# V loaded in place, scalings on ACT, f16 halves for the last keys, logits in two parts, fewer routing steps, and a new order of all queues

## The chip, the cores and the metric

The kernel runs on one core of a Trainium2 chip. The metric is the device time of one execution in microseconds. The engines are PE (matmuls; PEld is its loading of weights), DVE (vector), ACT (scalar, activations), POOL (GpSimd) and SP (which issues most DMAs). Each runs its own instructions in order and waits on semaphores for the others.

## The reference

```python
scores = scale * np.matmul(q, k.transpose(0, 1, 3, 2))     # 8 batches, 8 heads, 576 tokens, 64 wide
kth = np.partition(scores, -top_k, axis=-1)[..., -top_k:-top_k + 1]      # top_k = 32
scores = np.where(scores >= kth, scores, -1000000000.0)
attn = np.exp(scores - np.max(scores, axis=-1, keepdims=True))
attn = attn / (np.sum(attn, axis=-1, keepdims=True) + 1e-09)
x = np.matmul(attn, v)                                     # then (8*576, 512)
logits = x @ w_gate                                        # 8 experts
order = np.argsort(-logits.flatten())
for idx in order:                                          # cap = 4608 / 8 = 576
    tok, e = (int(idx) // E, int(idx) % E)
    if assigned[tok] >= 0 or counts[e] >= cap:
        continue
    assigned[tok] = e
    counts[e] += 1
...
out[mask] = np.maximum(x[mask] @ w1[e], 0.0) @ w2[e]       # mask: the tokens of expert e
```

## The kernel before

**Attention.** The work is 32 pairs: a batch and two neighbouring heads. A pair has 2 x 576 queries in nine tiles of 128: tiles 0 to 3 are the first head's first 512 queries, 5 to 8 the second head's, and tile 4 the last 64 queries of both. q and k are scaled and split into an f16 high and low part, so that two f16 matmuls give scores near f32. `prep` does this for a pair ahead: loads (SP), scaling (`scaled`), high and low parts (POOL), transposes by DMA (`turn`, four a pair: K2, K3, Q2, Q1), and for V a load, `scaledv`, `highv` (ACT) and `lowerv` (POOL).

`tile_ops` finds each query's 32nd largest score: PE writes the scores into one of three PSUM buffers `s`; DVE takes the eight largest of each of six pieces of 96 (L221) and from those, in five steps, the first 24 (L224 to L228); `sign` on ACT marks the scores above the 24th and sums the marks into `acc`; PE adds a large number there (`move(off)`); DVE fills eight more columns (`fill`, L238) and takes the next eight (`next8`, L239); PE moves the scores back (`move(back)`); `relu` on ACT leaves a mask that frees the buffer.

`soft` makes the weights for one tile, keys on the partitions: mask and scores again on PE, `expo` on ACT, f16 high and low parts on POOL (L293, L296). These cover the first 512 keys. `tail` does the last 64 keys for eight tiles at once (`E4`) and the corner of the last queries and last keys (`E4r`). `values` multiplies with V, whose column 65 of constants gives the sum; one group of tiles at a time, of tile 4 with f32 weights. A division on DVE and a scaling on ACT write x. After the four pairs of a batch, `logits` transposes x and multiplies with the gate, and x goes to DRAM.

The order of each engine's queue is set by `Plan`, a list scheduler: every operation has a due time (`O`, with a distance `PER` a tile), an assumed duration `d`, and a window for each engine (`WIN`). What it chooses becomes the program's order; on the chip each engine keeps it. `verdict` then sums checks of `acc`, `cuts` and the logits into `flags`; a branch skips the repair `redo`.

**Experts.** `moe()` uses a second plan. Expert by expert, a search finds the threshold above which the chosen expert has 576 tokens: six steps of comparing on DVE (`g`, L671), counting on PE (L674), adding up (L677, L680, L684), comparing with 576 (`okb`, L687) and taking the best expert (L688, L689). Then the tokens are listed (`enlist`), gathered from DRAM (`bring`: POOL gathers, ACT and DVE split into f16 parts, SP transposes by DMA into `xT`), and two layers of matmuls follow (L856, L880), while the next experts are routed and their weights `wr` loaded by SP and split by ACT and DVE. The first search is `p==0`.

Of the kernel before, what the change touches and what calls it, by code (L numbers as in the profile page):

```python
# [99 lines left out]
def attention(tc, q,k,v,w_gate,x_out,L,flags, pairs):  # L100
# [3 lines left out]
    with ExitStack() as ctx:  # L104
# [37 lines left out]
        O=dict(ld=-16.716, hk=-154.219, hq=68.962, gk=-25.585, gk2=47.53, gq=-130.711, gq2=-89.008, tk=27.44, tk3=-68.629, tq=-75.928, lv=6.408, hv=31.03, gv=101.34, gv2=-15.258, S=-52.406, c0=108.15, c1=-33.761, c2=85.771, c3=-0.645, c4=16.105, c5=34.028, nt=11.747, wb=-7.377, k0=-35.533, k1=-46.672, k2=-51.349, k3=-28.446, k4=23.429, nb=22.884, sg=24.883, wm=-11.243, y8=-71.884, j8=28.216, rl=-16.239, m1=-12.137, m2=-85.93, q2=64.018, t0=37.709, t1=91.29, t2=-2.439, td=-2.756, ex=108.922, eh=53.858, el=35.874, u0=34.296, ud=-71.623, ue=-103.988, uh=-45.573, ul=-62.63, x0=29.098, xe=-69.485, xh=-60.222, xl=9.443, v0=45.124, v1=49.568, v2=49.224, vd=-1.065, vn=-40.84, vs=19.481, lg=53.386, lgd=6.924, l1=-50.298, l2=2.231, l3=-3.333, hg=96.246)  # L142
# [4 lines left out]
        def prep(n):  # L147
# [53 lines left out]
            P["lds"]=at(t0+O["lv"],loadv,[l],e="D",d=2.2,late=2.0)  # L201
            P["vs"]=s3=at(t0+O["gv"],scaledv,[P["lds"],q2]+p3,e="G",d=.95)
            a=at(t0+O["hv"],lambda: highv(0),[s3],e="A",d=.3); a=at(t0+O["hv"]+O["hg"],lambda: highv(1),[a],e="A",d=.3)
            P["vready"]=at(t0+O["gv2"],lowerv,[a],e="G",d=1.13)
        def tile_ops(P,i):
# [32 lines left out]
            def fill(): V.tensor_scalar(D["s"][:,576:584],tab,acc[:,col],P["st"][:,i,23:24],op0=ALU.is_lt,op1=ALU.mult)  # L238
# [21 lines left out]
            if i%3==2:  # L260
                i0=i-2
                def most():
                    t=wk.tile([128,3],F32,tag="m3",name="m3",bufs=2)
                    G.tensor_scalar(t,P["st"][:,i0:i0+3,0],1.0/QS,0.0,op0=ALU.mult,op1=ALU.add)
                    G.tensor_scalar(P["nq"][:,1,i0:i0+3,64],t,1.0,0.0,op0=ALU.mult,op1=ALU.add)
                    G.tensor_tensor(P["nq"][:,1,i0:i0+3,65],t,P["nq"][:,1,i0:i0+3,64],op=ALU.subtract)
                def q2(): nc.sync.dma_start_transpose(P["Q2t"][:,i0:i0+3,:],P["nq"][:,1,i0:i0+3,:].rearrange("p a b -> p (a b)"))
                a=at(t0+O["m1"],most,[P["mx"][j] for j in range(i0,i+1)],e="G",d=.6); P["q2"][i0//3]=at(t0+O["q2"],q2,[a],e="D",d=.65,late=2.0)
        def soft(P,i):
# [27 lines left out]
            p=tp=at(t0,masks,[P["rel"][i],P["q2"][i//3]],take="pt",e="P",d=.225)  # L297
# [12 lines left out]
        def tail(P):  # L310
# [36 lines left out]
        def values(P):  # L347

            n=P["n"]; hp=P["hp"]; last=[]
            for g in (0,1,2):  # L350
# [4 lines left out]
                def dot(j,part,D=D,g=g,begin=begin):  # L355
                    if j==0 and part==0: begin()
                    av=D["av"]; vt,vh,vl=P["vt"],P["vh"],P["vl"]
                    h=0 if g==0 else 1
                    if g!=1: e_=P["e"][j if h==0 else 5+j]; out=av[:,j,:]; cs=lambda c: slice(c*128,c*128+128); last=P["e4"][:,j*128:j*128+128]
                    else: h=j; e_=P["e"][4]; out=av[h*64:h*64+64,0,:]; cs=lambda c: slice(c*128+h*64,c*128+h*64+64); last=P["e4r"]  # L360
                    if type(e_) is tuple: seq=[(e_[x][:,cs(c)],v_[:,h,c,:]) for c in range(4) for (x,v_) in ((0,vh),(0,vl),(1,vh))]
                    else: seq=[(e_[:,cs(c)],vt[:,h*5+c,:]) for c in range(4)]
                    seq.append((last,vt[:,h*5+4,:])); N=len(seq)
                    for m_ in (range(N-1) if part==0 else (N-1,)): T.matmul(out,seq[m_][0],seq[m_][1],start=(m_==0),stop=(m_==N-1))  # L364
# [23 lines left out]
        def logits(P):  # L388
            b=P["b"]; n=P["n"]; t0=(n*9+8)*PER+O["lg"]
            fin=[]  # L390
            for c in range(5):
                p=P["done"]
                D={}; w=512 if c<4 else 256
                def turn(c=c,D=D):
                    D["pt"]=ps_t.tile([128,512],F32,tag="pt",name="ptl")
                    for f in range(4 if c<4 else 2): T.transpose(D["pt"][:,f*128:(f+1)*128],P["x"][0][:,c,f*128:(f+1)*128] if c<4 else P["x"][1][:,2*f:2*f+2,:].rearrange("p a d -> p (a d)"),identf)
                def copy(D=D,w=w):
                    D["xT"]=wk.tile([128,512],F32,tag="xT",name="xT",bufs=2); A.activation(D["xT"][:,:w],D["pt"][:,:w],AF.Copy)
                def dot(c=c,D=D):
                    lg=D["lg"]=ps_t.tile([128,512],F32,tag="pt",name="lg"); xT=D["xT"]; o=(b%2)*64  # L400
                    if c<4:
                        for f in range(4): T.matmul(lg[:,:8],xT[:,f*128:(f+1)*128],wg[:,f,:],start=(f==0),stop=(f==3))
                    else:
                        for i_,(g,a) in enumerate(((0,0),(0,1),(1,0),(1,1))): T.matmul(lg[o:o+64,:8],xT[:,g*128+a*64:g*128+a*64+64],wgr[:,g,a,:],start=(i_==0),stop=(i_==3))
                def put(c=c,D=D):
                    o=(b%2)*64
                    if c<4: A.activation(L[:,b*4+c,:],D["lg"][:,:8],AF.Copy)
                    else: A.activation(L[o:o+64,32+b//2,:],D["lg"][o:o+64,:8],AF.Copy)
                t=t0+O["lgd"]*c
                p=at(t,turn,[p],take="pt",e="P",d=.436); tp=p  # L410
                p=at(t+O["l1"],copy,[p],free=[tp],take="xT",e="A",d=.48); tx=p
                p=at(t+O["l2"],dot,[p],take="pt",free=[tx],e="P",d=.9); tp=p
                p=at(t+O["l3"],put,[p],free=[tp],e="A",d=.07); fin.append(p)
            P["fin"]=at(t0,lambda: None,fin)
            P["done"]=p
        def verdict():

# [531 lines left out]
```

## Time and profile before

| | |
|---|---|
| median of 3 runs | 1474.12 us (1472.0 to 1474.5) |
| the profiled execution | 1470.44 us, its span 1468.4 us |
| granted TensorE clock, mean | 0.958 |
| PE busy | 1295.9 us (88%) |
| DVE busy | 1220.3 us (83%) |
| ACT busy | 864.6 us (59%) |
| POOL busy | 877.2 us (60%) |

Busy times are sums over three stages with different limits: attention up to about 955 us, routing up to 1028 us, and experts behind it. The rows below are from stretches of one stage.

### The profile page before, as it was taken

The page shows a single profiled execution, that of the slowest core. Times are in us where ns is not written, and L with a number is a line of the kernel's source. Part 1 is how long each engine was busy: PE and PEld are TensorE (multiplying, and loading weights), DVE is VectorE, ACT ScalarE, POOL GpSimd, SP SyncE. Part 2 cuts the span into 40 slices and gives each one's busy share as a digit, 9 for nine tenths or more (in the row PEclk, how much of TensorE's full clock was granted, in tenths as well). Part 3 has the DMA queues.
Part 4 walks back from the last instruction along what each step waited for, and adds up shares of the span by engine and source line. Part 5 has one row for each costly group of instructions (what it writes and reads, how often), then busy time and mean ns, then how long its engine had stood idle before and what let it go on. Part 6 is the DMA issues. An engine that isn't in the chain of part 4 may idle for free. (4 is left out here: it accounts for less than half of the span.)

```text
span 1468.4 us, 41338 instructions
## 1 busy us (share of the span) xinstructions
PE 1295.9 (88%) x14885; PEld 913.2 (62%) x14886; DVE 1220.3 (83%) x5951; ACT 864.6 (59%) x1922; POOL 877.2 (60%) x1285
## 2 busy tenths in 40 slices
PE   2888998999999999999999899832999999998997
PEld 1666776776776776677677677621655655664663
DVE  4899999999999999999999999658889878887610
ACT  2677777777777777777777787612334424324421
POOL 5688789788788788789879878502043123122211
PEclk9899999999999999999999999955999999999899
DMA  6343363354455445443543452016346346348500
GB/s 130 74 88 78 80 127 84 75 120 91 82 110 97 89 108 84 94 109 77 97 110 83 92 107 46 10 35 170 122 99 198 137 91 198 140 96 271 112 33 33
DMA packets 298149, 149.62 MB, mean 102 GB/s; under 512 B 255440, under 2 KB 280016, under 8 KB 296912
## 3 DMA queue, kind: packets, MB, share of 16 engines
q1 hardware_dynamic: 292048, 128.02, 38.5%
q0 software_dynamic: 5888, 18.88, 4.5%
q8 instruction: 119, 1.95, 0.6%
q14 instruction: 94, 0.77, 0.2%
HBM read 71.34 MB, written 18.87 MB: 61 GB/s over the span
## 5 line engine op out<-in xcount | busy, mean ns | idle before, releaser
L221 DVE MAX8 cd<-s 128x8 f32<-128x96 f32 x1728 | 383.2, 251 | 35.4 <-PE s L218 28.6
L296 POOL TENSOR_TENSOR elm<-F,ehm 128x512 f16<-128x512 f32 x256 | 294.3, 1156 | 6.3
L242 ACT ACTIVATE r<-s,st 128x576 bf16<-128x576 f32 x288 | 213.0, 740 | 98.8 <-PE s L236 93.8
L233 ACT ACTIVATE w<-s,st 128x576 uint16<-128x576 f32 x288 | 213.1, 740 | 95.0 <-DVE st L229 92.9
L895 POOL DMA_INDIRECT out_dram<-ob,idx x40 | 59.0, 1476 | 326.1 <-ACT ob L890 268.2
L239 DVE MAX8 st<-s 128x8 f32<-128x584 f32 x288 | 220.5, 766 | 10.4 <-PE s L236 6.7
L218 PE MATMUL s<-K,Q 128*128 128x512 f16 (+3 forms) x1280 | 195.3, 293 | 28.6 <-DMA Q<-nq 22.3
L856 PE MATMUL ph<-xT,w1h 128*128 128x288 f16 x1024 | 195.8, 289 | 2.0 <-DMA xT<-xs 2.0
L293 POOL TENSOR_SCALAR ehm<-F 128x512 f16<-128x512 f32 x256 | 156.0, 617 | 52.7 <-ACT F L290 52.3
L286 PE MATMUL pt<-Q,K 66*128 66x128 f16 (+1 forms) x1280 | 182.6, 217 | 0.2 <-DMA Q<-nq 0.2
L285 PE MATMUL pt<-Q,K 128*128 128x128 f16 (+1 forms) x1280 | 181.6, 216 | 0.0
L218 PEld LDWEIGHTS <-Q 128*128 128x128 f16 (+1 forms) x1280 | 105.9, 103 | 111.9 <-DMA Q<-nq 22.0
L236 PE MATMUL s<-w,off 128*128 128x512 f16 x576 | 134.1, 290 | 46.8 <-DVE s L238 26.9
L290 ACT ACTIVATE F<-pt 128x512 f32<-128x512 f32 x256 | 150.4, 596 | 20.8 <-PE pt L286 18.5
L856 PE MATMUL ph<-xT,w1l 128*128 128x288 f16 x512 | 147.6, 288 | 0.0
L364 PE MATMUL pv<-vt,E 128*64 128x65 f32 (+1 forms) x1024 | 146.4, 257 | 0.0
L236 PE MATMUL s<-w,back 128*128 128x512 f16 x576 | 120.9, 292 | 23.5 <-DVE st L239 21.7
L865 ACT ACTIVATE hh<-ph 128x288 f16<-128x288 f32 x128 | 52.4, 410 | 146.3 <-PE ph L856 145.4
L285 PEld LDWEIGHTS <-K 128*128 128x128 f16 x1280 | 118.3, 99 | 22.5 <-issue 8.7
L364 PEld LDWEIGHTS <-ehm 128*128 128x128 f16 x2048 | 116.2, 102 | 10.0 <-issue 0.5
L364 PEld LDWEIGHTS pv<-vt,E 128*64 128x64 f32 (+1 forms) x1024 | 113.0, 164 | 14.5 <-issue 3.5
L364 PE MATMUL pv<-vh,ehm 128*128 128x65 f16 x1024 | 120.8, 195 | 0.6 <-ACT F L290 0.6
(252 smaller groups left out, 3271.0 us busy)
## 6 DMA issues: line engine op xcount, KB each, us to landing
wr<-in_moe_w_dram SPq DMA_DIRECT2D x32, 1024.0 KB, 8.2
kn<-in_k_dram SPq DMA_DIRECT2D x64, 128.0 KB, 2.6
qn<-in_q_dram SPq DMA_DIRECT2D x64, 128.0 KB, 2.3
vn<-in_v_dram SPq DMA_DIRECT2D x64, 128.0 KB, 2.3
x<-xb SPq DMA_DIRECT2D x8, 1024.0 KB, 4.8
Q<-nq SPq DMA_TRANSPOSE x160, 3.3
kn<-in_k_dram SPq DMA_DIRECT2D x64, 16.0 KB, 2.3
qn<-in_q_dram SPq DMA_DIRECT2D x64, 16.0 KB, 2.2
```

The lines of the kernel that those rows point to most:

```text
L218: T.matmul(s_ps[rows,a:b_],P[Q][:,qc],P[K][:,h*576+a:h*576+b_],start=(Q=="Q1"),stop=(Q=="Q2"))
L221: V.max(D["cd"][:,c*8:c*8+8],D["s"][:,576*c//NCH:576*(c+1)//NCH])
L233: A.activation(D["w"],D["s"][:,:576],AF.Sign,bias=P["st"][:,i,32:33],scale=(1+2.0**-21),accum_out=acc[:,col])
L236: T.matmul(D["s"][:,a:b_],by,w[:,a:b_],start=False,stop=True,skip_group_check=True)
L239: def next8(): V.max(P["st"][:,i,24:32],D["s"][:,:584])
L242: A.activation(r,D["s"][:,:576],AF.Relu,bias=P["st"][:,i,31:32],scale=-1.0)
L285: T.matmul(o,K2[:,kb:kb+128],Q1[:,qc],start=False,stop=False,skip_group_check=True)
L286: T.matmul(o,K3[0:66,kb:kb+128],Q2[0:66,qc],start=False,stop=(c==3 and h==sub[-1][0]),skip_group_check=True)
L293: G.tensor_scalar(D["eh"],D["E"],1.0,0.0,op0=ALU.mult,op1=ALU.add)
L296: G.tensor_tensor(el,D["E"],D["eh"],op=ALU.subtract); P["e"][i]=(D["eh"],el)
L364: for m_ in (range(N-1) if part==0 else (N-1,)): T.matmul(out,seq[m_][0],seq[m_][1],start=(m_==0),stop=(m_==N-1))
L856: P.matmul(B["ph"][:,:288],a[:,c,fs],xT[:,b+c,cs],start=(i==0),stop=(i==11))
```

## The change

- V is loaded straight into `vt`, whose rows hold 65 floats, without a buffer of its own; its scaling, in place, and those of q and k go from POOL to ACT. `vh` and `vl` now hold all ten blocks.
- The weights of the last 64 keys are split into f16 high and low parts on POOL and multiplied by three f16 matmuls; before, one f32 matmul did it. The f32 weights share the ring `F`. In tile 4 the two heads' f32 matmuls alternate.
- `fill` multiplies by a constant instead of a column.
- `logits` is split: three of four column blocks after a batch's third pair, the rest after the fourth; the results are put, and added, by DVE. `verdict` looks at the logits in four pieces.
- In the first search the counts of all thresholds come from PE directly, without L677, L680 and L684. In all searches a constant row in `okb` takes the place of the matmul with `mone` (L685).
- For the first expert, `bring` transposes on PE and writes `xT` from PSUM by ACT and DVE, instead of by DMA.
- `PER`, `SP`, `WIN` and `O` have new values in both plans, so that the order of all queues is another.

```diff
-        PER=4.6166; SP=1.3822; VP=3; WPB=14; EHB=14
-        WIN={'V': 0.027, 'A': 0.079, 'G': 0.008, 'P': 0.138, 'D': 1.472}
+        PER=3.6791; SP=5.5328; MG=3; WPB=14; EHB=14
+        WIN={'V': 0.009, 'A': 0.159, 'G': 0.0, 'P': 0.097, 'D': 2.593}
...
             def loadv():
-                t=nat["v"]=io.tile([128,9,64],F32,tag="vn",name="vn")
                 for h in range(2):
-                    nc.sync.dma_start(out=t[:,h*4:h*4+4,:],in_=v[b,2*hp+h,0:512,:].rearrange("(p c) d -> p c d",c=4))
-                    nc.sync.dma_start(out=t[64*h:64*h+64,8,:],in_=v[b,2*hp+h,512:576,:])
...
+                    nc.sync.dma_start(out=vt[:,h*5:h*5+4,0:64],in_=v[b,2*hp+h,0:512,:].rearrange("(p c) d -> p c d",c=4))
+                    nc.sync.dma_start(out=vt[64*h:64*h+64,h*5+4,0:64],in_=v[b,2*hp+h,512:576,:])
+            def scaledv(): A.activation(vt[:,:,0:64],vt[:,:,0:64],AF.Copy,scale=VS)
+            def highv(h): A.activation(vh[:,h*5:h*5+5,0:64],vt[:,h*5:h*5+5,0:64],AF.Copy)
+            def lowerv(): G.tensor_tensor(vl[:,:,0:64],vt[:,:,0:64],vh[:,:,0:64],op=ALU.subtract)
...
-                G.tensor_scalar(s,nat[nm],QS,0.0,op0=ALU.mult,op1=ALU.add)
+                A.activation(s,nat[nm],AF.Copy,scale=QS)
...
-            P["lds"]=at(t0+O["lv"],loadv,[l],e="D",d=2.2,late=2.0)
-            P["vs"]=s3=at(t0+O["gv"],scaledv,[P["lds"],q2]+p3,e="G",d=.95)
...
+            P["lds"]=lv=at(t0+O["lv"],loadv,[l]+p3,e="D",d=2.2,late=2.0)
+            P["vs"]=s3=at(t0+O["gv"],scaledv,[lv],e="A",d=.66)
...
-            def fill(): V.tensor_scalar(D["s"][:,576:584],tab,acc[:,col],P["st"][:,i,23:24],op0=ALU.is_lt,op1=ALU.mult)
+
+            def fill(): V.tensor_scalar(D["s"][:,576:584],tab,acc[:,col],2.0**40,op0=ALU.is_lt,op1=ALU.mult)
...
+            p=te=at(t0+O["u0"]+O["ue"],expo4,[p],free=[tp],take="F",e="A",d=.48)
+            p=P["te4"]=at(t0+O["u0"]+O["uh"],hi4,[p],take="E4",e="G",d=.59)
+            P["e4op"]=at(t0+O["u0"]+O["ul"],lo4,[p],free=[te],e="G",d=1.115)
...
-                    seq.append((last,vt[:,h*5+4,:])); N=len(seq)
...
+                        else: seq=[(P["e4"][x][:,js],v_[:,h*5+4,:]) for (x,v_) in ((0,vh),(0,vl),(1,vh))]
+                        for m_,(a,b_) in enumerate(seq): T.matmul(out,a,b_,start=(part==0 and m_==0),stop=(part==1 and m_==2))
+                    else:
+
+                        e_=P["e"][4]
+                        for c in range(5):
+                            for h in range(2):
+                                a=e_[:,c*128+h*64:c*128+h*64+64] if c<4 else P["e4r"]
+                                T.matmul(av[h*64:h*64+64,0,:],a,vt[:,h*5+c,:],start=(c==0),stop=(c==4))
...
+            if P["hp"]==2: logits(P,0)
+            if P["hp"]==3:
+                P["done"]=at(P["done"]["t"]+.001,lambda: None,[P["done"],Ps[n-1]["fin"]])
...
+                            if p==0:
+                                for j in range(q*n,q*n+n): P.matmul(D_["pn"][:T,:E],D_["g"][:,j,:],D_["ohb"][:,j,:],start=(j==0),stop=(j==NT-1))
...
-                        P.matmul(D_["pn"][:,16:16+E],onesb[:1,:],mone,start=True,stop=False,skip_group_check=True)
...
+                if p==0:
+                    B={}
+                    def turn(j=j,n=n,B=B):
+                        if j==0: e["xT"]=new(sm,[128,8,CAP],F16,"xT")
+                        B["pt"]=new(ps,[128,512],F32,"ph",4).rearrange("p (f n) -> p f n",f=4)
+                        for f in range(4): P.transpose(B["pt"][:,f,:n],xgs[j][:n,f*128:f*128+128],ident[:n,:n])
+                    def hi(j=j,n=n,B=B): A.activation(e["xT"][:,0:4,j*128:j*128+n],B["pt"][:,:,:n],AF.Copy,scale=SX)
+                    def lo(j=j,n=n,B=B): V.scalar_tensor_tensor(e["xT"][:,4:8,j*128:j*128+n],B["pt"][:,:,:n],SX,e["xT"][:,0:4,j*128:j*128+n],op0=ALU.mult,op1=ALU.subtract)
```

Three places of the new order follow. On PE, in `values` of one pair in the middle of the attention stage (`E` are tile 4's f32 weights, `E4` and `E4r` those of the last keys, `s` a tile's scores), there stood:

```order
L236 MATMUL s_18398<-w_18526,off_144 128x512
L364 MATMUL pv_18479<-vt2_185,E4_18323 128x65
L364 MATMUL pv_18576<-vt2_185,E_18217 64x65 x4
L236 LDWEIGHTS off_144
L236 MATMUL s_18398<-w_18526,off_144 128x64
L364 MATMUL pv_18576<-vt2_185,E4r_18354 64x65
L364 MATMUL pv_18576<-vt2_185,E_18217 64x65 x4
L236 LDWEIGHTS back_146
L236 MATMUL s_18398<-w_18526,back_146 128x512
```

The same work in a pair of the change:

```order
L370 LDWEIGHTS eh4_11893
L370 MATMUL pv_12081<-vh1_183,eh4_11893 128x65
L370 LDWEIGHTS eh4_11893
L370 MATMUL pv_12081<-vl1_187,eh4_11893 128x65
L370 LDWEIGHTS el4_11900
L370 MATMUL pv_12081<-vh1_183,el4_11900 128x65
L377 MATMUL pv_12182<-vt1_179,E_11743 64x65 x8
L377 MATMUL pv_12182<-vt1_179,E4r_11971 64x65 x2
L231 LDWEIGHTS off_144
L231 MATMUL s_12002<-w_12194,off_144 128x512
```

The f32 matmul with `E4` has become three f16 ones with their weight loads, and tile 4's ten f32 calls stand in one piece; before, moves of a tile stood between them.

On DVE, at the end of the attention stage (`vc` to `good` are the check of `acc`, `fin` that of the logits `L`), the order before was:

```order
L424 SCALAR_TENSOR_TENSOR vok<-vc,vok 128x288
L425 SCALAR_TENSOR_TENSOR vok<-vc,vok 128x288
L426 SCALAR_TENSOR_TENSOR vok<-cuts,vok 128x288
L428 TENSOR_REDUCE good<-vok 128x32
L430 TENSOR_TENSOR fin<-L 128x288
```

And in the change:

```order
L428 COPY L<-lg 64x8
L432 TENSOR_TENSOR L<-lg,L 128x32
L433 TENSOR_TENSOR L<-lg,L 64x8
L439 TENSOR_SCALAR vc<-acc 128x288
L440 TENSOR_SCALAR vr<-vc 128x288
L441 TENSOR_SCALAR vr<-vr 128x288
L442 TENSOR_TENSOR vok<-vr,vc 128x288
L443 SCALAR_TENSOR_TENSOR vok<-vc,vok 128x288
```

The logits' puts are now on DVE, and they stand ahead of the eight instructions that check `acc`.

On SP, at the last experts (`wr` are weights, `xT<-xs` the transposes of expert 6's input), the order before was:

```order
L787 DMA wr<-in_moe_w_dram 128x2x1024
L840 DMA_TRANSPOSE xT<-xs 128x8x128
L787 ISA
L787 DMA wr<-in_moe_w_dram 128x4x512
L840 DMA_TRANSPOSE xT<-xs 128x8x128 x3
L840 DMA_TRANSPOSE xT<-xs 128x8x64
```

And in the change:

```order
L819 DMA wr<-in_moe_w_dram 128x2x1024
L885 DMA_TRANSPOSE xT<-xs 128x8x128 x2
L819 ISA
L819 DMA wr<-in_moe_w_dram 128x4x512
L885 DMA_TRANSPOSE xT<-xs 128x8x128 x2
L885 DMA_TRANSPOSE xT<-xs 128x8x64
```

One more of the five transposes stands ahead of the load of weights.

## Rows read from the trace of the kernel before

**Rows 1.** Busy us of PE, PEld, DVE, ACT, POOL (instructions) in a stretch of attention

```profile
400.00:600.00 200.00, 185.62 (x2541) 139.65 (x2540) 187.93 (x1054) 153.85 (x361) 170.81 (x264) 0.99 0.49 97
```

**Rows 2.** One line's instructions, `clear` of each pair: durations, first and last start

```profile
L308 POOL TENSOR_SCALAR cuts<-st x32: 202/212/216, 57.6 to 941.7; 128x9 f32<-128x9 f32 x32
```

**Rows 3.** Waits from 200 to 800 us: total us, times, longest

```profile
DVE cd L221 <- PE s L218: 7.2, 20, 1.2
...
DVE s L238 <- PE s L236: 2.5, 10, 0.3
DVE st L239 <- PE s L236: 2.5, 8, 0.4
...
PE pt L286 <- DMA Q<-nq: 0.2, 1, 0.2
```

**Rows 4.** Timeline of PE in `values`: start us, us, instruction

```profile
948.11 0.41 PE L364 MATMUL pv<-vt,E 128*128 128x65 f32 x2
948.37 0.19 PE L364 MATMUL pv<-vh,ehm 128*128 128x65 f16 x1
...
948.73 0.41 PE L364 MATMUL pv<-vt,E 128*128 128x65 f32 x2
```

**Rows 5.** Timeline of PE in tile 4's values, both heads' halves

```profile
927.17 0.22 PE L364 MATMUL pv<-vt,E4r 128*64 128x65 f32 x1
927.18 0.57 PE L364 MATMUL pv<-vt,E 128*64 128x65 f32 x7
```

**Rows 6.** Groups from 200 to 800 us, each engine's: busy us, mean ns

```profile
L238 DVE TENSOR_SCALAR s<-tab,acc,st 128x8 f32<-128x8 f32 x189 | 53.1, 281 | 5.9 <-PE s L236 2.5 <-ACT w L233 1.1
L344 DVE TENSOR_SCALAR rs<-pv 128x4 f32<-128x4 f32 (+1 forms) x63 | 9.2, 145 | 0.9
L290 ACT ACTIVATE F<-pt 128x512 f32<-128x512 f32 x169 | 99.3, 596 | 12.4 <-PE pt L286 11.3 <-POOL elm L296 0.4 <-POOL vt L170 0.3
L177 POOL TENSOR_SCALAR sc<-kn 128x576 f32<-128x576 f32 x21 | 14.1, 672 | 0.0
```

**Rows 7.** DMA issues: times, KB each, median us to landing

```profile
vn<-in_v_dram SPq DMA_DIRECT2D x64, 128.0 KB, 2.3
x<-xr SPq DMA_DIRECT2D x16, 64.0 KB, 4.7
```

**Rows 8.** Timeline of SP's queue at the start

```profile
16.64 0.59 SPq L158 DMA_DIRECT2D kn<-in_k_dram  x1
...
19.00 1.33 SPq L186 DMA_TRANSPOSE Q<-nq  x1
```

**Rows 9.** Timeline of DVE in the check; idle before and its releaser in brackets

```profile
954.31 0.29 DVE L420 TENSOR_SCALAR vc<-acc 128x288 f32<-128x288 f32 x1
...
957.36 0.45 DVE L428 TENSOR_REDUCE good<-vok 128x32 f32<-128x288 f32 x1
...
964.14 0.46 DVE L430 TENSOR_TENSOR fin<-L 128x288 f32<-128x288 f32 x1 [6.33 <-ACT L L408]
...
967.13 0.14 DVE L443 CAST flags<-bad 1x1 int32<-1x1 f32 x1
```

**Rows 10.** Timeline of DVE in the last step of the first search

```profile
997.30 0.19 DVE L677 TENSOR_TENSOR cm<-pc,dm 128x32 f32<-128x32 f32 x1 [0.23 <-PE pc L674]
...
998.10 0.15 DVE L687 TENSOR_SCALAR okb<-pc 32x8 bf16<-32x8 f32 x1 [0.37 <-PE pc L685]
```

**Rows 11.** Timeline of ACT and PE at the first gather

```profile
1022.02 0.63 ACT L836 ACTIVATE xs<-xg 128x512 f16<-128x512 f32 x1 [0.47 <-DMA xg<-x,idx]
...
1027.87 0.64 PE L856 MATMUL ph<-xT,w1h 128*128 128x288 f16 x2 [2.00 <-DMA xT<-xs]
```

**Rows 12.** Timeline of PE among the experts' matmuls

```profile
1123.08 0.17 PE L685 MATMUL pc<-mone,onesb 1*128 1x8 bf16 x1
1123.19 0.39 PE L880 MATMUL po<-w2h,hh 128*128 128x512 f16 x1
```

**Rows 13.** Waits of PE from 1028 to 1462 us

```profile
PE pl L765 <- DVE bt L761: 8.1, 1, 8.1
```

More of the change, by code (lines that the diff above doesn't have):

```diff
@@ L387, in store @@
                 nc.sync.dma_start(out=x_out[b*576+512:b*576+576,:].rearrange("t (g r d) -> t g r d",r=2,d=64)[:,:,par,:],in_=xr[par*64:par*64+64])
[L388 to L397, printed above, removed]
-                    D["xT"]=wk.tile([128,512],F32,tag="xT",name="xT",bufs=2); A.activation(D["xT"][:,:w],D["pt"][:,:w],AF.Copy)
[L399 to L415, printed above, removed]
@@ L432, in verdict @@
-            V.tensor_reduce(good[:,npr:],fin,axis=AX.X,op=ALU.add)
+            whole=[]
+            for k,(u0,u1) in enumerate(((0,28),(32,35),(28,32),(35,36))):
+                Lf=L[:,u0:u1,:].rearrange("p t e -> p (t e)"); w=8*(u1-u0); fin=cp.tile([128,w],F32,name=f"fin{k}")
+                V.tensor_tensor(fin,Lf,Lf,op=ALU.subtract)
+                V.tensor_scalar(fin,fin,0.0,None,op0=ALU.is_equal)
+                V.tensor_reduce(good[:,npr+k:npr+k+1],fin,axis=AX.X,op=ALU.add); whole.append(128.0*w)
@@ L433, in verdict @@
             ones=cp.tile([128,1],F32,name="ones1"); V.memset(ones,1.0)
+            want=cp.tile([1,npr+4],F32,name="want"); V.memset(want[:,:npr],1152.0)
+            for k,x_ in enumerate(whole): V.memset(want[:,npr+k:npr+k+1],x_)
             pt=ps_t.tile([128,512],F32,tag="pt",name="ptv")
-            T.matmul(pt[:1,:npr+1],ones,good,start=True,stop=True)
-            bad=cp.tile([1,npr+1],F32,name="bad"); V.tensor_copy(bad,pt[:1,:npr+1])
-            V.tensor_scalar(bad[:,:npr],bad[:,:npr],-1.0,1152.0,op0=ALU.mult,op1=ALU.add)
@@ L438, in verdict @@
-            V.tensor_scalar(bad[:,npr:],bad[:,npr:],-1.0,128.0*Lf.shape[1],op0=ALU.mult,op1=ALU.add)
-            V.tensor_scalar(bad[:,:npr],bad[:,:npr],bad[:,npr:],None,op0=ALU.add)
+            T.matmul(pt[:1,:npr+4],ones,good,start=True,stop=True)
+            bad=cp.tile([1,npr+4],F32,name="bad"); V.tensor_tensor(bad,want,pt[:1,:npr+4],op=ALU.subtract)
+            nf=cp.tile([1,1],F32,name="nf"); V.tensor_reduce(nf,bad[:,npr:],axis=AX.X,op=ALU.add)
+            V.tensor_scalar(bad[:,:npr],bad[:,:npr],nf,None,op0=ALU.add)
@@ L608, in moe @@
         pen=cp.tile([128,E],F32,name="pen"); V.memset(pen,0.0)
+        okbs=[cp.tile([T+1,E],BF16,name=f"okb{k}") for k in range(2)]
+        for t in okbs: V.memset(t[T:T+1,:],-1.0)
         U=cp.tile([128,NT],F32,name="U"); V.memset(U,1.0)
@@ L673, in count @@
                         def count(q=q):
-                            for j in range(q*n,q*n+n,4): P.matmul(D_["pc"][:,:32],D_["g"][:,j:j+4,:].rearrange("p a b -> p (a b)"),D_["ohb"][:,j:j+4,:].rearrange("p a b -> p (a b)"),start=(j==0),stop=(j==NT-4))
-                        mms.append(plan.at(c.t,count,cv+(mms[-1:]),e="P",d=.03*(n//4)+.03))
-                    c.pre=[mms[-1]]; c.t+=.15
-                    c.add("V",.10,lambda: V.tensor_tensor(o("cm",128,32),D_["pc"][:,:32],dm,op=ALU.mult))
@@ new lines, in route, with fold, total @@
+                        mms.append(plan.at(c.t,count,cv+(mms[-1:]),e="P",d=.03*(n//4)+.03 if p else .03*n+.03))
+                    c.pre=[mms[-1]]; c.t+=.15
+                    if p:
+                        c.add("V",.10,lambda: V.tensor_tensor(o("cm",128,32),D_["pc"][:,:32],dm,op=ALU.mult))
+                        def fold():
+                            o("ch",128,E,dt=F16)
+                            with nc.allow_low_precision(reason="counts up to 1152"): V.tensor_reduce(D_["ch"],D_["cm"].rearrange("p (j e) -> p e j",e=E),axis=AX.X,op=ALU.add)
+                        c.add("V",.10,fold)
+                        def total():
+                            D_["pn"]=new(ps,[128,512],F32,"pc",1)
+                            P.matmul(D_["pn"][:T,:E],sel_,D_["ch"],start=True,stop=True)
+                        c.add("P",.06,total)
```

139 lines of the change are left out of this document (83 added, 56 removed).

## The prediction

> **What bounds the kernel now.** I read the busy times by stretch first, then the pace of the pairs, then the waits, then single places in the timeline. In the attention stage PE works 185.62 us of 200 and DVE 187.93, ACT 153.85 and POOL 170.81 [rows 1]: two engines are nearly full at once, so neither alone is the bound. One small POOL instruction that runs once a pair gives the pace: from 57.6 to 941.7 us in 31 steps, 28.5 us a pair [rows 2], so 32 pairs take 912 us. DVE has 12.07 us free in 200, or 1.72 us a pair. The waits of 600 us of this stage say for what DVE waits: PE's scores 7.2, PE's moves 2.5 and 2.5, in all 12.2 us, 2.0% of the time; PE waits for a transfer for 0.2 us only [rows 3]. The rest of DVE's free time is not put down to another engine. After the attention stage come chains in which one engine waits for the other: the last logits and the check [rows 9], the search of the routing [rows 10], the first gather [rows 11]. From 1027.87 us PE runs the experts without a gap but for one wait of 8.1 us [rows 13].
>
> **The attention stage, PE.** An f32 matmul of the last 64 keys' weights holds PE from 948.11 to 948.37, 0.26 us; the twelve f16 ones behind it go from 948.37 to 948.73, 0.03 each [rows 4]. Three f16 in its place take 0.09, so 0.17 is saved, eight times a pair: 1.3 us. In tile 4, f32 calls of one half follow each other at 0.08 us (seven in 0.57), while one of the other half starts 0.01 ahead of its neighbour [rows 5]. The twenty records of a pair take about 1.6 us in a row; if all run two by two, half, 0.8. I take 0.6 (bounds 0, where the mixture in the row shows that some already do, and 0.8). PE loses 1.9 us of 26.5 a pair.
>
> **DVE.** `fill` costs 281 ns nine times a pair; a TENSOR_SCALAR with constants 145 [rows 6]. It loses one of two column operands: 0 to 0.136 us each, I take 0.06, nearer the first since one operand stays; 0.54 a pair. The logits' puts come to DVE, seven in four pairs at the same 145 ns: 0.26. DVE gains 0.28, of which I count 0.2, 6.4 us over 32 pairs (bounds -31 from 9 x 0.136 less 0.26, and +8).
>
> **What PE's relief gives.** DVE's waits for PE, 2.0% of 912 us, are 18.5 us. PE will still work 24.6 of 28, so I let half go: 9.3 us (bounds 0 and 18.5). With DVE's own, 16 us for the stage.
>
> **ACT and POOL.** POOL's scaling of k takes 672 ns, and q's the same; both, and V's, leave it, and the two conversions of the last keys' weights come to it. I cost the balance at nothing: among the waits of DVE and PE none names POOL. ACT takes the scalings: 512 columns take 596 ns [rows 6], so 576 about 0.65 and V's 640 about 0.7, in all 2.0 us a pair, less 0.2 for the puts; it goes from 21.9 to 23.7 us of 28. That is covered by ACT's free time as long as no sign or relu that DVE wants next stands behind such a piece; the price without that cover is the last rival's.
>
> **V's load.** V now lands in rows of 65 floats, in pieces of 256 bytes. The nearest transfer with such pieces, x from xr, takes 4.7 us for 64 KB where V's old one took 2.3 for 128 KB [rows 7]. By size that makes 4.7 to 9.4 us. V is wanted a pair's length after its load, 28 us, so I cost it at nothing; K's and Q's transposes stand behind it on SP, and PE hardly waits for those now. The Trainium skill, DMA: Bandwidth & Descriptors, Specifications, asks for at least 512 B a piece and says that smaller ones are read, modified and written; it speaks against this load. By that page the load lands late, as by the row, and the sum stays as long as the cover does; the weight of the rule is in the chance of a slower result. Whether it holds for pieces into the core's own memory no run here shows; the row is of pieces that go out.
>
> **The order of all queues** is new. No row prices it. The bounds are DVE's whole free time, -55 us (32 x 1.72), and the last rival's +61; I take 0, since the loop of a tile (scores, maxima, sign, move, maximum, move, relu) has the same steps.
>
> **Start.** Q's second transpose leaves SP at 19.00, behind four loads of k that begin at 16.64 [rows 8]; now it goes ahead of them. That is worth 0 to 2.4 us, less V's longer issue ahead of it; I take 1.
>
> **End of the attention stage.** Before, the check's eight instructions on the counts ran from 954.31 to 957.81 under the logits; the logits ended near 964.1 and the rest of the check lay at 964.14 to 967.27, 3.1 us [rows 9]. Five pieces in 9.8 us are 2 us each. Now two pieces are left at the end, overlapping: about 3 us, to 957.3 (up to 958.2 without overlap). That looks like a gain of 6, but DVE's queue has the last puts ahead of the eight instructions, 3.5 us, which now lie behind the logits; then 3.1, and nine more small ones at about 0.16, 1.5. The flags come at 965.4 to 966.3: a gain of 1 to 1.9, I take 1.5.
>
> **Routing.** In a step of the first search, from 997.30 to 998.10 two DVE instructions and PE's sum stand between the counting matmuls and the comparison [rows 10]. They go, 0.8 us; 36 narrow matmuls in place of nine add up to 0.3 to 0.8 at the end of each part. I take 0.5 a step, six steps: 3 us (bounds 0 and 4.8).
>
> **First gather.** ACT reads the third block at 1022.02; the first FFN matmul waits for the transposed copy until 1027.87, 5.85 us [rows 11]. Now four PE transposes of about 0.6, ACT 0.63 and a DVE piece of 0.7, with the steps between, are some 2.25: 3.6 us less (bounds 0, if DVE's queue holds the piece back, and 4.5).
>
> **Experts.** The removed matmul stands 0.11 us on PE, from 1123.08 to 1123.19 [rows 12]; of the later six searches' 36, nearly all lie in PE's full stretch: 3 of 4.0 us counted. The wait of 8.1 us [rows 13] came as expert 7's list waited for a DVE instruction that stood behind the last block of expert 6's input, and that behind four transposes which SP held back behind a load of weights. SP now issues two of the five ahead of that load; PE, on the other side, comes to the list 2.6 us earlier. I take half, 4 (bounds +2.6 and -8.1).
>
> **Sum.** 16 + 1 + 1.5 + 3 + 3.6 + 3 + 4 = 32.1 us off the profiled execution's 1470.4: 1438.3. The median of the runs shown is 1474.1, 3.7 above; in its terms 1442.
>
> **Rivals.**
> First, the stage keeps its pace: DVE works 187.93 of 200, its instructions nearly all remain, and what waits for PE today waits for the next thing in the queue. For it speaks that PE and DVE hand the same tile to each other four times, against it the 12.2 us in the waits. Then only the ends gain, 16.1: 1458.
>
> Second, more goes: PE late is also what lies behind waits that carry other names, and the new order lets DVE run nearly full. All its free time, 55, and 6 for its own, and the ends' 16: 1397; two thirds of the free time: 1415.
>
> Third, slower, by ACT. Its queue holds relu and sign of each tile, for which PE and DVE wait next; three pieces of 0.65 us a pair now stand among them. If each delays in full a tile that DVE wants next, that is 1.9 us a pair, 61 over the stage: 1442 + 61 = 1503. Against it speaks that ACT is free for 46 us of 200 and three tiles are in flight. It makes the kernel slower from a delay of 1.1 us a pair (32.1 + 2.9 over 32). The Trainium skill, Perfetto Trace Analysis, in its part on TensorE's phases says that ACT, DVE and GPSIMD are strict FIFO, so that by it a piece that is not urgent holds up what is behind it. The trace agrees so far that in the experts DVE's instructions stand in the queue behind one that waits [rows 13].
>
> Fourth, the expert stage does not gain: the wait stays or grows by 2.6, 1449. It moves the time inside the range only, so it has no chance of its own.
>
> **Numbers.** A change of 0.2% (2.9 us) is about what a measurement of this kernel can tell. Forecast 0.47; the pace stays 0.18; more goes 0.18; gains and losses cancel 0.05; slower 0.12, of which 0.03 is for V's load, should its 2.4 to 7.1 us of longer landing (4.7 to 9.4 for 2.3) reach Q's transposes. Faster is 0.47 + 0.18 + 0.18 = 0.83. The range runs from 1405, which leaves out the far third of the second rival, 0.06, to 1472, which leaves out the slower one: 0.18 outside.
>
> **What would show it.** Pace: the POOL instruction once a pair at 28.0 us apart. PE's busy time in 200 us near 176 with DVE still at 187, and its waits for PE at half. ACT's scalings beside idle time, no new wait of DVE for sign or of PE for relu. In tail and routing: flags about 11 us behind the last division, a search step near 3.05 us, first FFN matmul some 2.3 us after ACT reads the third block less hops. The wait in the experts at 4 us. The prediction falls if the pace is 28.5 or more, or under 27.3.

## The result and the profile after

| | before | after |
|---|---|---|
| median | 1474.31 us (4 runs) | 1458.28 us (4 runs, 1456.19 to 1459.63) |
| ratio, 95% interval | | 0.9887, 0.9862 to 0.9912 |
| the profiled execution's span | 1468.4 us | 1456.5 us |

The change is 1.1% faster, 16 us; 32 were forecast, in a range that holds the result. 1458 is the time that the first rival gave, whose claim was an unchanged pace. The two profiled executions lie 12 us apart, as the one before was 3.9 under its median. They show where the two spans part, in us from the start of each:

| up to | before | after | this stretch | forecast |
|---|---|---|---|---|
| end of the first pair (POOL's instruction once a pair) | 57.6 | 54.0 | -3.6 | -1 |
| the same of the last pair | 941.7 | 935.6 | -2.5 | -16 |
| the flags | 967.1 | 957.2 | -3.8 | -1.5 |
| the first expert is chosen | 999.2 | 986.3 | -3.0 | -3 |
| the first FFN matmul | 1027.9 | 1013.8 | -1.2 | -3.6 |
| the last FFN matmul's end | 1458.7 | 1447.1 | +2.5 | -7 |

The pace first: the line of POOL that runs once a pair.

```profile
L304 POOL TENSOR_SCALAR cuts<-st x32: 208/213/227, 54.0 to 935.6; 128x9 f32<-128x9 f32 x32
```

31 steps in 881.6 us are 28.44 a pair, where [rows 2] gave 28.52. Busy times by stretch (PE, PEld, DVE, ACT, POOL, as in [rows 1]):

```profile
200.00:400.00 200.00, 174.24 (x2571) 127.50 (x2569) 183.36 (x1059) 164.51 (x375) 165.49 (x239) 0.99 0.49 92
400.00:600.00 200.00, 175.76 (x2627) 128.34 (x2626) 188.03 (x1084) 170.67 (x389) 170.85 (x243) 1.00 0.50 100
600.00:800.00 200.00, 171.80 (x2527) 125.96 (x2527) 180.27 (x1045) 161.48 (x367) 162.97 (x236) 0.98 0.49 97
```

PE has lost its 10 us in 200, yet DVE too works less in the first and last stretch, not more. So something new holds both up. The waits of 200 to 800 us, which answer to [rows 3], name it:

```profile
PE pt L282 <- DMA Q<-nq: 18.0, 14, 2.3
...
DVE st L235 <- PE s L231: 10.6, 19, 2.7
DVE cd L216 <- PE s L213: 10.1, 23, 1.4
DVE s L234 <- PE s L231: 9.3, 14, 2.2
```

PE waits 18.0 us for a transposed Q where it waited 0.2, and DVE 30.0 for PE where it waited 12.2. One such place in the timeline:

```profile
657.39 0.60 SPq L158 DMA_DIRECT2D kn<-in_k_dram  x1
...
657.69 0.20 POOL L262 TENSOR_TENSOR nq<-m,nq 128x3 f16<-128x3 f32 x1
...
659.77 2.65 SPq L181 DMA_TRANSPOSE K<-nk  x1
...
662.46 1.25 SPq L263 DMA_TRANSPOSE Q<-nq  x1
...
666.21 0.27 PE L282 MATMUL pt<-Q,K 66*128 66x128 f16 x1 [2.30 <-DMA Q<-nq]
...
668.11 0.78 DVE L235 MAX8 st<-s 128x8 f32<-128x584 f32 x1 [2.70 <-PE s L231]
```

POOL has the row maxima of three tiles ready at 657.89 (L260 to L262 in `most`). Their DMA transpose (L263) stands on SP behind the next pair's loads of k and a transpose of K, and goes out at 662.46, 4.6 us late. From the starts and ends of these rows, such a transpose left SP 0.3 us after POOL's part in the kernel before, on average between 200 and 800 us, and 1.8 at most; in the changed kernel it is 1.7 on average, and 14 of 63 are over 3 us late. PE comes to the matmul that needs it (`soft`), stands there 2.30 us, and behind it in PE's queue stand the moves of a tile for whose maximum DVE waits 2.70 us.

The end of the stage, on DVE, beside [rows 9]:

```profile
945.60 0.18 DVE L390 RECIPROCAL rs<-rs 128x4 f32<-128x4 f32 x1
...
949.36 0.17 DVE L433 TENSOR_TENSOR L<-lg,L 64x8 f32<-64x8 f32 x1
949.55 0.31 DVE L439 TENSOR_SCALAR vc<-acc 128x288 f32<-128x288 f32 x1
...
952.99 0.38 DVE L451 TENSOR_TENSOR fin<-L 128x224 f32<-128x224 f32 x1
...
957.24 0.16 DVE L465 CAST flags<-flf 1x32 int32<-1x32 f32 x1
```

The logits end at 949.5, then come 3.4 us of the check on the counts, then 4.4 to the flags: 11.6 us behind the last division where it had been 12.9 (from the row here to the 967.27 of [rows 9]):

```profile
954.23 0.16 DVE L378 RECIPROCAL rs<-rs 128x1 f32<-128x1 f32 x1
```

The first gather, beside [rows 11]:

```profile
1000.50 5.70 POOL L861 DMA_INDIRECT xg<-x,idx  x1 [55.77 <-DMA wr<-in_moe_w_dram]
1004.48 0.67 DVE L839 SCALAR_TENSOR_TENSOR w1l<-wr,w1h 128x512 f16<-128x512 f32 x1
1006.51 0.97 POOL L861 DMA_INDIRECT xg<-x,idx  x1 [0.30 <-issue]
...
1008.61 1.12 PE L871 MATMUL ph<-identm,xg 128*128 128x128 f32 x4 [7.42 <-DMA xg<-x,idx]
...
1010.44 0.69 DVE L873 SCALAR_TENSOR_TENSOR xT<-ph,xT 128x512 f16<-128x512 f32 x1 [5.29 <-ACT xT L872]
...
1011.58 1.12 PE L871 MATMUL ph<-identm,xg 128*128 128x128 f32 x4 [0.42 <-issue]
...
1013.84 0.69 PE L901 MATMUL ph<-xT,w1h 128*128 128x288 f16 x2
```

The first two gathers of the kernel before were these:

```profile
1013.51 1.44 POOL L829 DMA_INDIRECT xg<-x,idx  x1 [62.87 <-PE pc L688]
1015.26 2.35 POOL L829 DMA_INDIRECT xg<-x,idx  x1 [0.31 <-issue]
```

POOL's first gather takes 5.70 us where it took 1.44, the second 0.97 where it took 2.35. And the waits of PE from there to the end, beside [rows 13]:

```profile
PE pc L705 <- DVE g L699: 3.9, 3, 3.0
PE po L925 <- DVE ob L939: 2.1, 1, 2.1
...
PE pl L797 <- DVE bt L793: 0.3, 1, 0.3
```

The wait of 8.1 us has shrunk to 0.3. But the ten rows of PE's waits in this stretch add up to 12.1 us, where the kernel before had five rows and 13.4 us: the 8.1, 2.0 at the first matmul, 0.2, and these two:

```profile
PE pc L674 <- DVE g L671: 1.8, 4, 1.0
PE pc L684 <- DVE ch L680: 1.3, 1, 1.3
```

### The profile page after: what moved, and what is told of

Read it like the earlier page. It is cut to its first block, busy times and chain, and to the rows that moved or that the text cites. A ratio compares the mean times of both kernels' runs of the same rounds, so it can differ in the third digit from the quotient of the medians.

```text
span 1456.5 us, 42268 instructions
## 1 busy us (share of the span) xinstructions
PE 1244.9 (85%) x15275; PEld 853.7 (59%) x15276; DVE 1202.5 (83%) x6016; ACT 919.6 (63%) x1994; POOL 870.4 (60%) x1189
## 5 line engine op out<-in xcount | busy, mean ns | idle before, releaser
L216 DVE MAX8 cd<-s 128x8 f32<-128x96 f32 x1728 | 376.9, 252 | 32.6 <-PE s L213 30.2
L235 DVE MAX8 st<-s 128x8 f32<-128x584 f32 x288 | 220.6, 766 | 15.3 <-PE s L231 12.9
L213 PE MATMUL s<-K,Q 128*128 128x512 f16 (+3 forms) x1280 | 191.9, 290 | 29.4 <-DMA Q<-nq 21.4
L282 PE MATMUL pt<-Q,K 66*128 66x128 f16 (+1 forms) x1280 | 178.6, 215 | 21.8 <-DMA Q<-nq 21.7
L231 PE MATMUL s<-w,off 128*128 128x512 f16 x576 | 137.7, 288 | 66.6 <-DVE s L234 51.3
L940 POOL DMA_INDIRECT out_dram<-ob,idx x40 | 55.4, 1384 | 221.4 <-ACT ob L935 154.3
L861 POOL DMA_INDIRECT xg<-x,idx x40 | 51.9, 1297 | 175.6 <-DVE idx L807 107.7
L370 PE MATMUL pv<-vl,ehm 128*128 128x65 f16 x1024 | 121.7, 194 | 0.0
L370 PE MATMUL pv<-vh,elm 128*128 128x65 f16 x1024 | 121.3, 194 | 0.0
```

The source lines that it names most:

```text
L213: T.matmul(s_ps[rows,a:b_],P[Q][:,qc],P[K][:,h*576+a:h*576+b_],start=(Q=="Q1"),stop=(Q=="Q2"))
L216: V.max(D["cd"][:,c*8:c*8+8],D["s"][:,576*c//NCH:576*(c+1)//NCH])
L231: T.matmul(D["s"][:,a:b_],by,w[:,a:b_],start=False,stop=True,skip_group_check=True)
L235: def next8(): V.max(P["st"][:,i,24:32],D["s"][:,:584])
L282: T.matmul(o,K3[0:66,kb:kb+128],Q2[0:66,qc],start=False,stop=(c==3 and h==sub[-1][0]),skip_group_check=True)
L370: for m_,(a,b_) in enumerate(seq): T.matmul(out,a,b_,start=(part==0 and m_==0),stop=(part==1 and m_==2))
```

## The experiments

The changed kernel is meant where no other is named. The ratios are to the kernel before on the same chip. Theory A for the stage: the change made room on PE and DVE, and the late transposes took it. Its rival B: the steps of a tile set the pace whatever PE has free.

**Transposes of the maxima early.** The plan's sequence is kept; only this operation is written into the program right behind POOL's part, so that SP's order alone changes.

```diff
+            for o in op["next"]:
+                if o["soon"] and all(id(p) in done for p in o["pre"]): emit(o)
...
-P["q2"][i0//MG]=at(t0+O["q2"],q2,[a],e="D",d=.65,late=2.0)
+P["q2"][i0//MG]=at(t0+O["q2"],q2,[a],e="D",d=.65,late=2.0,soon=True)
```

> The changed kernel; on SP alone the DMA transposes of the row maxima (three tiles at a time) are issued as soon as POOL's part ahead of them stands in the program; the order of PE, DVE, ACT and POOL is the changed kernel's row for row. Theory A (the gain of the attention stage went into PE's new wait for these transposes, 18.0 us between 200 and 800): the wait falls under 5 us, the pace from 28.4 to 27.6 to 28.0 us a pair, the time from 1458 to 1431 to 1446. Theory B (the steps of the tile between DVE and PE set the pace and the wait only took the place of another): the wait falls too, the pace stays at 28.3 to 28.5 and the time at 1454 to 1460.

Measured: 1439.44 us, ratio 0.9769 (0.9747 to 0.9790). The pace, busy times and the wait:

```profile
L312 POOL TENSOR_SCALAR cuts<-st x32: 203/212/221, 53.7 to 916.7; 128x9 f32<-128x9 f32 x32
```

```profile
400.00:600.00 200.00, 177.65 (x2702) 130.18 (x2702) 190.06 (x1101) 171.49 (x392) 172.79 (x246) 1.00 0.52 104
```

```profile
DVE cd L224 <- PE s L221: 8.2, 21, 1.6
DVE s L242 <- PE s L239: 4.3, 13, 0.4
...
DVE st L243 <- PE s L239: 1.8, 11, 0.2
PE pt L290 <- DMA Q<-nq: 1.4, 3, 0.5
```

The wait is 1.4 us, the pace 27.84, the stage 19 us shorter (863.0 us from the first pair to the last, where it was 881.6), DVE busy 190 of 200 and waiting 14.3 us for PE. In the trace the instructions of PE, DVE, ACT and POOL stand in the changed kernel's order throughout; SP's alone differs. A holds, and B falls.

**`fill` alone.** The kernel before with the constant in place of the column.

```diff
-V.tensor_scalar(D["s"][:,576:584],tab,acc[:,col],P["st"][:,i,23:24],op0=ALU.is_lt,op1=ALU.mult)
+V.tensor_scalar(D["s"][:,576:584],tab,acc[:,col],2.0**40,op0=ALU.is_lt,op1=ALU.mult)
```

> The kernel before with one edit: fill multiplies by a constant, in the same order of all queues. It takes 0.06 us from DVE 288 times, 17 us. Theory A (DVE's own work and its waits for PE add up, DVE is the stage's bound): 12 to 17 us faster than before, 1457 to 1462. Theory B (the path through a tile's buffers sets the pace, DVE has slack): at most 5 us, 1469 to 1476.

Measured: 1461.57 us, ratio 0.9920 (0.9897 to 0.9942): 11.8 us for 17 us of DVE's work, and a pace of 28.12.

```profile
L308 POOL TENSOR_SCALAR cuts<-st x32: 202/212/217, 58.3 to 930.0; 128x9 f32<-128x9 f32 x32
```

This is just under A's 12 us and far over B's 5: about seven tenths of the cut in DVE's own work arrive already in the kernel before.

**Last keys in f32 again.**

```diff
-seq=[(P["e4"][x][:,js],v_[:,h*5+4,:]) for (x,v_) in ((0,vh),(0,vl),(1,vh))]
+seq=[(P["e4"][:,js],vt[:,h*5+4,:])]
```

> The changed kernel with the last 64 keys' weights in f32 again (their two POOL conversions left out, one f32 matmul in place of three f16), else the same order. PE gets 1.3 us a pair back, 42 us over the stage. If PE's relief is on the path (theory A): 10 to 40 us slower than the changed kernel, 1468 to 1498. If PE has slack as it stands (theory B): 1456 to 1462.

Measured: 1471.14 us, ratio 0.9975 (0.9960 to 0.9991), 13 us slower. PE's relief is on the path. The wait for the transposes is 1.3 us here: PE comes later, and they are in time. So the next run puts both together.

**Last keys in f32, transposes early.**

> The kernel with early transposes and the last keys' weights in f32 (no POOL conversions for them); the same order. Without early transposes this form took 1471 and already had only 1.3 us of that wait. Theory A (PE's relief is on the path and the late transposes had hidden it): 1464 to 1473, 25 to 34 slower than with f16. Theory B (its slowness came from the late transposes): 1445 to 1458.

Measured: 1470.38 us, ratio 0.9988 (0.9974 to 1.0002).

```profile
L312 POOL TENSOR_SCALAR cuts<-st x32: 202/212/222, 53.9 to 946.0; 128x9 f32<-128x9 f32 x32
```

The early transposes give nothing to a PE that comes late. Against 0.9769 this is 0.022 of 1474, 32 us, for the f16 halves in this order; PE's saving was put at 42. In the form as changed 13 of these had arrived (0.9975 to 0.9887); the rest had gone into the new wait. Both f32 forms keep an order that was fitted to the f16 halves, so what the halves are worth in an order of their own is not shown.

**Early transposes, `fill` with the column.**

> The kernel with early transposes of the maxima, and fill takes the column again; the same order. DVE gets 0.06 us 288 times, 17 us. Theory A (with PE relieved, DVE's own work sets the pace): 1450 to 1457. Theory B (a wait still hides some of it): 1440 to 1447.

Measured: 1453.22 us, ratio 0.9868 (0.9844 to 0.9892): 0.0099 above 0.9769, 14.6 us for 17 of DVE's work.

```profile
L312 POOL TENSOR_SCALAR cuts<-st x32: 201/213/218, 54.8 to 927.0; 128x9 f32<-128x9 f32 x32
```

The time is A's, but only part of it is the pace: 28.14 us a pair against 27.84, 9 us over the stage. The rest of the difference lies in small pieces outside it, the first gather among them. So between a half and six sevenths of DVE's own work show in the time; what hides the rest is open.

**Scaling of q and k on POOL, transposes early.**

```diff
-                A.activation(s,nat[nm],AF.Copy,scale=QS)
+                G.tensor_scalar(s,nat[nm],QS,0.0,op0=ALU.mult,op1=ALU.add)
```

> The kernel with early transposes of the maxima, and the scaling of q and k back on POOL at the same place of the program. ACT loses 1.35 us a pair and POOL gets it. Theory A (ACT has slack for the scalings, as the prediction had it): not faster than 1439, at POOL's cost up to 1450. Theory B (the rival: ACT's pieces hold up relu and sign on the path): faster, 1425 to 1436.

Measured: 1446.75 us, ratio 0.9822 (0.9795 to 0.9849), 7 us slower; theory A. That taking these two pieces off ACT makes the kernel faster, as the rival has it, falls. What they cost on ACT by themselves is not shown, since POOL gets busier by the same edit, and V's scaling was not tried.

**The old numbers for the order of routing and experts.** They take the place of the changed kernel's in `moe()`; the fewer steps stay.

```diff
-        O=dict(RT=341.23, TE=-289.219, TN=-172.671, WT=261.813, XT=32.643, RD=-297.654, GL=2.6, W_V=0.1, W_A=0.395, W_G=2.142, W_P=0.0, W_D=9.225, WD0=678.788, WD1=322.634, RA=-247.153, WT0=9.992, TE0=-55.559, XT0=-502.675)
+        O=dict(RT=274.437, TE=-46.447, TN=-90.531, WT=82.391, XT=-180.56, RD=-288.435, GL=2.6, W_V=0.099, W_A=2.033, W_G=0.144, W_P=0.0, W_D=0.747, WD0=757.588, WD1=237.776, RA=-374.027, WT0=-194.686, TE0=-40.731, XT0=-156.385)
```

> The changed kernel with the numbers that set the order of routing and experts taken from the kernel before; the fewer steps stay. Theory A (the new order of the experts costs about what the old wait of 8.1 us did, in new gaps of PE with a lower clock behind them): from the first FFN matmul to the end 424 to 429 us where the changed kernel has 433, time 1449 to 1455, unless the old wait of 8 us comes back (1457 to 1463). Theory B (the gaps come from the removed steps themselves): the same gaps, 1456 to 1461.

Measured: 1451.62 us, ratio 0.9844 (0.9825 to 0.9862), 6.7 us faster. From the first FFN matmul to the last, 427.3 us, where the changed kernel has 432.9 and the kernel before 430.4.

```profile
PE pl L797 <- DVE bt L793: 6.6, 1, 6.6
```

The old wait has come back, 6.6 us, and the stage is faster all the same, so A's sum (424 to 429) held without its condition. With the old numbers the stretch is 3.1 us shorter than before, as the fewer steps should make it; with the new ones it is 2.5 longer. One execution each stands behind these lengths.

**Both: early transposes, old expert numbers.**

> The changed kernel with both: the row maxima's transposes issued early on SP, and the old numbers for the order of routing and experts. If the two losses lie apart (theory A): 1439.4 less 6.6, 1430 to 1436. If one hid the other (theory B): 1437 to 1441.

Measured: 1430.77 us, ratio 0.9726 (0.9698 to 0.9754). The two losses lie apart: the old numbers take 0.0043 off the ratio with the early transposes (0.9769 to 0.9726) and without them (0.9887 to 0.9844), 6.3 us. In the profiled execution, the slowest but one of five at 1435.61 us, the stretch from the first FFN matmul to the last takes 432.5 us, where 427.3 were measured for the same order, so the lengths of single executions tell the experts' stage to about 5 us only. The attention stage takes 863.3 us (53.4 to 916.7), as in the first experiment.

**The check ahead of the last divisions**, on top of both: its eight DVE instructions become operations of the plan that follow the last pair's `clear`.

```diff
+        p_=[P["clear"]]
+        for f_ in steps(): p_=[at(9e9,f_,p_,e="V",d=.4)]
```

> As the kernel with both edits, and the check's eight instructions on the counts stand on DVE ahead of the last divisions and puts, else the same order. Theory A (they lay on the path of the end only by their place in DVE's queue): the flags come 3 to 3.5 us earlier after the last division, and the time is 2.5 to 3.5 us less than with both edits. Theory B (the logits' own path ends as late): 0 to 1 us less.

Measured: 1426.59 us, ratio 0.9693 (0.9668 to 0.9719), 4 us less, a little more than A's 2.5 to 3.5.

```profile
923.22 0.18 DVE L398 RECIPROCAL rs<-rs 128x4 f32<-128x4 f32 x1
...
931.43 0.16 DVE L462 CAST flags<-flf 1x32 int32<-1x32 f32 x1
```

The flags now stand 8.2 us behind the last division, 3.4 earlier than in the changed kernel; it was the place in DVE's queue.

**Inputs ahead of weights**, on top of the last: for expert 7 the later two loads stand behind expert 6's transposes.

```diff
-late=2.0+3.0*(k+1),order=ops[-1:])
+late=2.0+3.0*(k+1),order=ops[-1:]+([X[6]["x"][-1]] if p==7 and k>1 else []))
```

> As the kernel with the early check, and on SP the last two loads of expert 7's weights stand behind the transposes of expert 6's input; else the same order. Theory A (PE's wait of 6.6 us for expert 7's list comes from those transposes standing behind a load): the wait falls under 2 us, the time is 4 to 9 us less than with the early check. Theory B (the transposes are slow by themselves, or the weights then come late): within 2 us of it, with another wait on PE.

Measured: 1428.41 us, ratio 0.9694 (0.9668 to 0.9721): no change, and the wait for the list is still 6.1 us, where it was 8.1 with the early check.

```profile
1296.07 2.57 SPq L830 DMA_DIRECT2D wr<-in_moe_w_dram  x2
1303.21 13.36 SPq L896 DMA_TRANSPOSE xT<-xs  x5
...
1312.21 0.63 ACT L892 ACTIVATE xs<-xg 128x512 f16<-128x512 f32 x1 [5.52 <-DMA xT<-xs]
```

Five transposes with no load between them still take 13.4 us on SP, so the load between them was not what held them back, and A falls. In that time ACT stands 5.52 us before it can write the fourth block, since `xs` has three buffers and an earlier transpose must land first. So the transposes wait for their own landings; whether these were slow because of the two loads ahead is open.

**The lists due earlier**, on top of the early check.

```diff
-TE=-46.447
+TE=-289.219
```

> As the kernel with the early check; of the numbers for the order of routing and experts one, the due time of the lists, is the changed kernel's. Theory A (with the list due earlier, PE's wait of 8.1 us for expert 7's list goes, as in the changed kernel): 1418 to 1424. Theory B (the wait moves to another place of the experts): 1425 to 1432.

Measured: 1422.73 us, ratio 0.9665 (0.9645 to 0.9685), the fastest. The time is A's, the reason is not: the wait for the list only went from 8.1 to 5.5 us.

```profile
PE pl L808 <- DVE bt L804: 5.5, 1, 5.5
```

## Why the prediction was right in its range and half in its size

**The order at nothing: the step that failed.** The prediction took 0 for the new order of the queues, "since the loop of a tile has the same steps". The loop has, but what feeds it on SP had moved: the maxima's transposes. That cost 17 us by the ratios (0.9887 to 0.9769) and 19 in the profiled stage, about the whole difference of 16 to the forecast. With that one operation early the kernel takes 1439 us, where 1442 was forecast, though not by its parts: the stage gains 21 for 16, and from the first FFN matmul on nothing is gained where 7 was counted. The rival named for such a loss was ACT's queue, which was not it. The queue was SP's, and the 0.03 for V's load reaching Q's transposes looked at the right queue and the wrong neighbour.

That the range held is in part luck. The pace, 28.44 us, is nearly the 28.5 at which the prediction said that it falls, and DVE's waits for PE, forecast at half, more than doubled. That the time is the first rival's 1458 is luck too: outside the stage the profile gained 9 us, not that rival's 16, and the medians lie 4 us further apart than the profiles.

**PE's relief and `fill`: PE's own saving was right, what arrives of it was guessed.** PE's busy time was forecast at 176 of 200 and is 172 to 176, or 24.7 us a pair where 24.6 was forecast. Tile 4's alternating calls run from 940.74 to the next work at 941.47, 0.73 us, where 1.0 was forecast:

```profile
940.74 0.69 PE L377 MATMUL pv<-vt,E 128*64 128x65 f32 x16
...
941.47 0.11 PEld L370 LDWEIGHTS <-ehm 128*128 128x128 f16 x2
```

Of this, half of DVE's waits, 9.3 us, was counted for the time. In the new order, with the transposes early, the f16 halves are worth 32, so there more of DVE's time hangs on PE than the rows that name PE showed. `fill` was right to the hundredth:

```profile
L234 DVE TENSOR_SCALAR s<-tab,acc 128x8 f32<-128x8 f32 x189 | 41.7, 221 | 10.3 <-PE s L231 9.3
```

0.060 us less. Its 17 us, less 8 for the puts and some caution, were counted as 6.4; by the two experiments 9 to 15 of the 17 arrive. With f32 and the constant, the new order runs at 28.78 us a pair (the run with f32 and early transposes) and the old one at 28.12. So the rest of the change, its order among it, costs some 20 us there. An order fitted to other durations may be part of that; how it divides among order, V, puts and ACT is open. The two sums belong together: with the transposes early the whole stage gains 21 us (884.1 to 863.0), and what `fill` leaves of that, 6 to 12, is near the 9.3. So it is not shown that PE's relief was sized too small.

**V's load** landed in time, as forecast:

```profile
vt<-in_v_dram SPq DMA_DIRECT2D x64, 128.0 KB, 2.7
```

That is 2.7 us where the old load took 2.3 [rows 7], against bounds of 4.7 to 9.4. The Trainium skill, DMA: Bandwidth & Descriptors, Specifications, asks for 512 B a piece; for these loads the trace does not bear out a price beyond 0.4 us. The row of x from xr was a bad neighbour.

**Start and end.** The first pair gained 3.6 for 1; what gave the rest is open. From the last pair to the flags it was 3.8 for 1.5, of which the check and the logits behind the last division are 1.3, as worked out; the order of DVE's queue kept the rest of the gain back, as the run with the early check shows.

**Search: right.** A step takes 2.96 us (971.29 to 974.25 in the profile after) where it took 3.55: 0.59 less for 0.5, 3.0 us from the flags to the choice.

```profile
971.29 1.50 DVE L699 TENSOR_TENSOR g<-v,thr 128x384 bf16<-128x384 f32 x3
...
973.36 0.15 DVE L718 TENSOR_SCALAR okb<-pc 32x8 bf16<-32x8 f32 x1 [0.17 <-PE pc L703]
...
974.25 1.50 DVE L699 TENSOR_TENSOR g<-v,thr 128x384 bf16<-128x384 f32 x3
```

**First gather: a third.** From the third block's transposes on PE to the first FFN matmul it is 2.26 us (1011.58 to 1013.84), as worked out, though not by its terms: the transposes took 1.12 where 0.6 was put. But POOL's first two gathers took 6.7 us where they had taken 3.8, and PE waited 7.42 for the first. In the runs with the old expert numbers they took 3.8 again, and from the choice of the first expert to the first FFN matmul it was 24.6 to 24.7 us where the kernel before had 28.7: 4.0 less for the 3.6. So the term was right, and the new order lost most of it.

**Experts: wrong in sum.** The prediction read PE's stretch as "without a gap but for one wait of 8.1 us"; the rows behind it have three more lines, 3.3 us in all. The old wait is gone, but new ones of nearly the same sum came for it, and PE's busy time did not fall by the 3 us counted for the removed matmul: 420.5 us from the first FFN matmul to the last, where it was 419.0. With the old numbers for the order it is 415.8, and the stretch 5.6 us shorter. Stretches at a lower clock behind the waits, as in the last section, fit this; how much of it they make is open. The cause that the prediction gave for the old wait, transposes behind a load, did not hold where it was tried: with no load between them the wait was still 6.1 us.

## What to carry over

When a table of due times is changed, take the queues that only issue, SP above all, and look at what each small, late transfer now stands behind: it has a consumer in another engine's queue, and what that consumer holds up is the price. Where two engines are about 90% busy at once, a good part of a cut on either one arrived here (9 to 15 us of 17 for `fill`, 32 of 42 for the f16 halves). So a gain that does not show may have gone into a new wait, and here one row of the waits after named it. An order fitted to one form of the work need not fit another, so part and order are to be measured apart; here that was done in part only.

## What was unexpected of the hardware

Loads in pieces of 256 bytes into the core's memory took 2.7 us for 128 KB, while writes in such pieces out of it took 4.7 for 64 KB [rows 7]. A long wait of PE was paid twice in the two cases looked at (1 is the upper of the clock's two levels, 2.4 GHz, and 0.5 the lower, 1.2 GHz): after one of 2.98 us in the changed kernel the granted clock was 0.72 in the mean of the next 6 us, and after the 8.1 us of the kernel before 0.52:

```profile
1178.00:1184.00 6.00, 5.88 (x28) 2.32 (x28) 5.14 (x14) 0.00 (x0) 3.07 (x2) 0.72 0.23 44
```

```profile
1360.00:1366.00 6.00, 6.00 (x51) 3.53 (x49) 3.04 (x8) 1.23 (x3) 0.05 (x1) 0.52 0.68 218
```

The first gather on POOL took 1.44 to 5.71 us in different kernels for the same first block. DVE may have a part in it: all 27 gathers in the traces of this case that ran beside an idle DVE took 0.91 to 0.97 us, all that took over 1.2 ran while DVE was at work for about a third of the time or more, and in the profile after the one of 5.70 ended 1.05 us after DVE fell idle at 1005.15. Many beside a busy DVE took 0.95 too, so DVE's being busy alone does not explain it, and no run tried it.
